# A third output buffer, lent from the matrix products' PSUM banks, for the convolution tiles in a fused backward pass

## The chip, the core and the metric

The kernel runs on one core of a Trainium2 chip. Its time is that of one execution on the device in microseconds, and what is compared are medians of several executions. A profile comes from one more execution that the hardware profiler recorded; "the profile" and "the trace" below are of that one.

## What is computed

The reference is the vector-Jacobian product of a block with two branches that run on one layer-normed input. One is a long convolution over time (2048 steps, 1024 channels) with gates, the other a gated MLP with F = 3584:

```python
xn = layernorm(q)                                   # q: [1, 2048, 1024]
# convolution branch
k_shift = sum of k shifted by t steps times shift_k[:, 3 - t], t = 0..3
kv = k_shift * v
y  = irfft(rfft(kv, padded) * rfft(ssm_k, padded))[:S] + kv * ssm_D
A  = xn * y
# MLP branch
B  = (relu(xn @ W_gate) * (xn @ W_up)) @ W_down
out = q + A + B
# outputs: out and the gradients by q, k, v, shift_k, ssm_k, ssm_D, W_gate, W_up, W_down
```

The kernel returns ten tensors in bfloat16: the forward output and nine gradients.

## The kernel before

**Two recorders on one queue.** Class `LnMlp` writes down the MLP branch and class `ABranch` the convolution branch. Both are Python generators. `LnMlp` yields after each small group of matmuls, with the nanoseconds that the group is worth (1730 for eight 128x512 matmuls in the weight gradients). The loop at the end of the kernel function subtracts these from `left`, and whenever `left` is used up it lets the convolution branch record its next slot and adds the slot's own cost: 1900 in the first stage; in the weight gradients 1900 if the slot holds matmuls and 1250 if not (`SLOT`, `DENSE`, L529). So the order of TensorE's queue is fixed by a budget of nanoseconds and not by what is ready. `A_START` (L777) is what has to pass before the convolution branch begins.

**The stages.**

1. `hidden` (L1046): layer norm, then fourteen blocks (two halves of the rows, seven blocks of 512 columns of F). Each block has eight row tiles, for which gate, up and the gradient of the hidden layer are formed, 8 matmuls each (tiles `ps_g`, `ps_u`, `ps_h`). SyncE loads the blocks of weights (`wg`, `wu`, `wdT`) and stores `h_d` and `ug_d`, in one queue with the convolution's loads and stores.
2. `grad_down` (L1363, tiles `ps_d`) and `grad_in` (L1403, tiles `ps_w`): the weight gradients, sums over 16 row tiles. `gemm16` (L1317) makes one output tile of 16 matmuls and yields after 8 and after 16; its caller then records the copy to SBUF on ScalarE. In three places `four` (L1325) works on four output tiles at once.
3. `out_phase` (tiles `ps_o`): the forward output, from `wd` and transposed rows of the hidden layer (`hT`).
4. `grad_x` (tiles `ps_x`): the gradient by q.

**The convolution branch** runs beside stages 1 and 2. It takes eight groups of 128 channels one after another. Long transforms are done as two rounds of small matmuls with tables of sines (`R`, `FW` forwards; `IA`, `RB` backwards), a VectorE transpose (`flip`) between the rounds, and complex products on VectorE (`cmul`). `slots` (L626) yields pairs: what TensorE does in a slot, and what VectorE does. A run of convolution matmuls that stands between two matmuls of the MLP branch is called a pass below. The small matmuls use parts of the array side by side: `FW` and `RB` 64 rows by 32 columns, `IA` and `R` 32 by 64. Each pass fills one or more PSUM tiles, and ScalarE empties each of them into SBUF (`act`, L74; in the profile its line is L76, and that of the small matmuls L72).

**PSUM.** It has eight banks of 128x512 float32. The matrix products rotate through four single banks (pool `b_ps`, `ps_tile`, L834). The convolution has two tiles of two banks each (pool `a_ps`, tag `aps`), so a third tile waits until the first has been emptied. All its steps (`fwd1_filter`, `fwd1`, `fwd2`, `fwd2_pair`, `inv_a`, `inv_a_pair`, `inv_b`, `inv_b_chan`, `tap_sums`, L330 to L510) take their tiles from there, and a pass fills two of them (in `tap_sums` one).

When the convolution branch has ended, its SBUF is released and `open_right` loads `wd` for stage 3.

Of the kernel before, what the change touches and what calls it, by code (L numbers as in the profile page):

```python
# [12 lines left out]
F32 = mybir.dt.float32  # L13
# [35 lines left out]
class ABranch:  # L49
# [5 lines left out]
    def __init__(self, tc, pri, S, D, k, v, g, shift_k, ssm_k, ssm_D, xn_d, y_d, sk_d, out_gk, out_gv, out_gsk,  # L55
                 out_gh, out_gsD):
        assert S == 2048 and D % P == 0
        self.tc, self.nc, self.pri = tc, tc.nc, pri
        self.S, self.D, self.NG = S, D, D // P
        self.k, self.v, self.g, self.shift_k, self.ssm_k, self.ssm_D = k, v, g, shift_k, ssm_k, ssm_D  # L60
        self.xn_d, self.y_d, self.sk_d = xn_d, y_d, sk_d
        self.out_gk, self.out_gv, self.out_gsk, self.out_gh, self.out_gsD = out_gk, out_gv, out_gsk, out_gh, out_gsD
        self.pools, self.pin, self.dense, self.queue = [], False, False, []

    def pool(self, name, bufs, **kw):
        p = self.tc.alloc_tile_pool(name=name, bufs=bufs, **kw)
        self.pools.append(p)
        return p

# [260 lines left out]
    def fwd1_filter(self, st):  # L330

        B, hn = self.Bh, st["hn"]
        for k in range(2):
            for x in range(2):
                ps = self.ps.tile([P, 2, 512], F32, name="ps0", tag="aps")
                for b in range(2):
                    rows = slice(64 * x + 32 * b, 64 * x + 32 * b + 32)
                    for h in range(2):
                        self.mm(ps[64 * h:64 * h + 64, b], self.R[rows].rearrange("p a l -> p (a l)"),
                                hn[rows, h, 16 * k:16 * k + 16, :].rearrange("p c n -> p (c n)"))  # L340
                self.act(B[:, :, x, 8 * k:8 * k + 8],
                         ps[:].rearrange("p b (cp i n) -> p b cp n i", i=2, n=NB1))
            yield
# [7 lines left out]
    def fwd1(self, B, src):  # L351
        for r0 in range(0, 16, 8):
            for u in range(2):
                ps = self.ps.tile([P, 2, 8, 64], F32, name="ps1", tag="aps")
                for b in range(2):
                    rows = slice(64 * u + 32 * b, 64 * u + 32 * b + 32)
                    for h in range(2):
                        self.mm(ps[64 * h:64 * h + 64, b], self.R[rows].rearrange("p a l -> p (a l)"),
                                src[rows, r0:r0 + 8, 64 * h:64 * h + 64])
                self.act(B[:, :, :, u, r0:r0 + 8, :], ps[:].rearrange("p b r (cp i) -> p b cp r i", i=2))  # L360
            yield

    def fwd2(self, F, half):
        Bf = self.flp[:, half]
        for j0 in range(0, 4, 2):
            for j in range(j0, j0 + 2):
                ps = self.ps.tile([P, 2, 2, 2, 2, 64], F32, name="ps2", tag="aps")
                for ri in range(2):
                    for m in range(2):
                        for q in range(4):  # L370
                            for e in range(2):
                                rows, l = slice(64 * e, 64 * e + 64), 8 * q + 2 * j + m
                                self.mm(ps[32 * q:32 * q + 32, e, :, ri, m, :], self.FW[rows, l, ri, :],
                                        Bf[rows, l, :].rearrange("p (b c) -> p b c", b=2))
                self.act(F[:, 2 * j:2 * j + 2].rearrange("p e b i c -> p (e b i c)"),
                         ps[:].rearrange("p e b i m c -> p (e b i m c)"))
            yield

    def fwd2_pair(self):

        for j in range(4):
            ps = [self.ps.tile([P, 2, 2, 2, 2, 64], F32, name="ps2", tag="aps") for _ in range(2)]
            for m in range(2):
                for ri in range(2):
                    for q in range(4):
                        for e in range(2):
                            rows, l = slice(64 * e, 64 * e + 64), 8 * q + 2 * j + m
                            self.mm(ps[e][32 * q:32 * q + 32, m, :, :, ri, :], self.FW[rows, l, ri, :],
                                    self.flp[rows, :, l, :].rearrange("p k (b c) -> p b k c", b=2))
            for e in range(2):  # L390
                self.act(self.GK[:, 2 * j + e].rearrange("p b k i (m c) -> p (b k i) m c", m=2),
                         ps[e][:].rearrange("p m b k i c -> p (b k i) m c"))
            yield

# [26 lines left out]
    def inv_a(self):  # L421
        C, Q = self.Cg, self.GKV
        for j0 in range(0, 4, 2):
            ps = [self.ps.tile([P, 2, 2, 2, 2, 64], F32, name="ps3", tag="aps") for _ in range(2)]
            for j in range(2):
                for m in range(2):
                    for ri in range(2):
                        for q in range(4):
                            for e in range(2):
                                rows, x = slice(32 * q, 32 * q + 32), 2 * (j0 + j) + m  # L430
                                self.mm(ps[q // 2][64 * e:64 * e + 64, q % 2, j, m],
                                        self.IA[rows, x, ri].rearrange("p a n -> p (a n)"),
                                        Q[rows, 2 * (j0 + j) + e, :, ri, 64 * m:64 * m + 64],
                                        start=ri == 0, stop=ri == 1)
            for h in range(2):
                self.act(C[:, :, 2 * h:2 * h + 2, 2 * j0:2 * j0 + 4, :],
                         ps[h][:].rearrange("p q j m b (cp i) -> p (b cp) q (j m) i", i=2))
            yield

    def inv_a_pair(self):  # L440

        for j in range(4):
            ps = [self.ps.tile([P, 2, 2, 2, 2, 64], F32, name="ps3", tag="aps") for _ in range(2)]
            for m in range(2):
                for ri in range(2):
                    for q in range(4):
                        for e in range(2):
                            rows, x = slice(32 * q, 32 * q + 32), 2 * j + m
                            self.mm(ps[q // 2][64 * e:64 * e + 64, q % 2, m].rearrange("p k b c -> p b k c"),
                                    self.IA[rows, x, ri].rearrange("p a n -> p (a n)"),  # L450
                                    self.GK[rows, 2 * j + e, :, :, ri, 64 * m:64 * m + 64],
                                    start=ri == 0, stop=ri == 1)
            for h in range(2):
                self.act(self.Cs[:, :, 2 * h:2 * h + 2, 2 * j:2 * j + 2, :],
                         ps[h][:].rearrange("p q m k b (cp i) -> p (k b cp) q m i", i=2))
            yield

    def inv_b(self, st, key, half):
        dst, Cf = self.ttile(key), self.flp[:, half]
        st[key] = dst  # L460
        for j in range(2):
            ps = self.ps.tile([P, 2, 8, 64], F32, name="ps4", tag="aps")
            for q in range(4):
                for e in range(2):
                    rows, n0 = slice(64 * e, 64 * e + 64), 16 * (q // 2) + 8 * j
                    self.mm(ps[32 * q:32 * q + 32, e], self.RB[rows, e, :],
                            Cf[rows, n0:n0 + 8, 64 * (q % 2):64 * (q % 2) + 64])
            self.act(dst[:, 8 * j:8 * j + 8, :].rearrange("p r (h c) -> p r h c", h=2),
                     ps[:].rearrange("p h r c -> p r h c"))
        yield  # L470

    def inv_b_chan(self, st, half):
# [3 lines left out]
        for n0 in range(0, NB1, 16):  # L476
            ps = self.ps.tile([P, 16, 64], F32, name="ps5", tag="aps")
            for n in range(16):
                self.mm(ps[:, n, :], Cf[:, n0 + n, :], self.RB[:].rearrange("p h n -> p (h n)"))
            self.act(dv[:, :, n0:n0 + 16], ps[:].rearrange("p n2 n1 -> p n1 n2"))  # L480
# [17 lines left out]
    def tap_sums(self, st):  # L498

        gks, kp = st["gks"], st["kp"]  # L500
        ps = self.ps.tile([P, 2, 512], F32, name="ps6", tag="aps")
        pd = ps[:, 0, 0:P].rearrange("p (i c) -> p i c", i=4)
# [11 lines left out]
    def both(self, *fs):  # L514
# [3 lines left out]
        return go  # L518

# [11 lines left out]
    def steps(self):  # L531
# [25 lines left out]
        for st in self.sts:  # L557
            for p, d in self.slots(st, st["gi"]):
                self.run(p)
# [198 lines left out]

    def small_outputs(self):
# [17 lines left out]
A_START = 45_000  # L777


class LnMlp:  # L780
# [536 lines left out]
    def gemm16(self, ps, lhsT, rhs):  # L1317
        for st in range(self.ST):
            self.pri.pin(self.nc.tensor.matmul(ps[:], lhsT=lhsT(st), rhs=rhs(st), start=(st == 0),  # L1319
                                               stop=(st == self.ST - 1)))  # L1320
            if st % 8 == 7:
# [41 lines left out]
    def grad_down(self, xn_d, ug_d, h_d, out_wd):  # L1363
# [9 lines left out]
        for fb in range(self.FB):  # L1373
# [5 lines left out]
            for j in range(4):  # L1379
                self.pri.now()  # L1380
                if j - 1 in whole:
                    continue
                if j in whole:
# [4 lines left out]
                else:  # L1388
                    wo = [self.e2_tile("wo")]
                    for ob in range(2):  # L1390
                        ps = self.ps_tile("ps_d")
                        yield from self.gemm16(ps, lambda st: hs(st)[:, j * P:(j + 1) * P],
                                               lambda st: gn[st][:, ob * 512:ob * 512 + 512])
                        self.pri.pin(nc.scalar.copy(out=wo[0][:, ob, :], in_=ps[:]))
# [8 lines left out]
    def grad_in(self, ug_d, out_wg, out_wu):  # L1403
        nc, xn, nxt = self.nc, self.xn_nat, self.ugs
        turns = [(fb, w) for fb in range(self.FB) for w in (1, 0)]
        for k, (fb, w) in enumerate(turns):
# [3 lines left out]
            for dp in range(self.DT // 2):  # L1410
# [10 lines left out]
                else:  # L1421
                    wo = [self.e2_tile("wi")]
                    for d in range(2):
                        dc = 2 * dp + d
                        ps = self.ps_tile("ps_w")
                        yield from self.gemm16(ps, lambda st: xn[st][:, dc * P:(dc + 1) * P], sl)
                        self.pri.pin(nc.scalar.copy(out=wo[0][:, d, :], in_=ps[:]))
# [154 lines left out]
def kernel(  # L1582
# [42 lines left out]
    a.identA = b.ident  # L1625
# [66 lines left out]
```

## Time and profile before

| | us |
|---|---|
| median of four executions | 1880.68 (1880.13 to 1881.44) |
| the profiled execution | 1881.13 |
| its span, first to last instruction | 1879.4 |
| `hidden` (to 645.5) | 645.5 |
| `grad_down`, `grad_in` (to 1295.65) | 650.2 |
| `out_phase` (to 1483.07) | 187.4 |
| `grad_x` (to 1879.4) | 396.3 |
| first and last convolution matmul | 110.5 and 1224.1 |

The granted TensorE clock was 1.000 throughout. In the profile, a line such as `PE L72 MATMUL ps<-arena,IA 32*64 32x256 bf16 x32` reads: TensorE, line 72 of the kernel, a matmul from `arena` and `IA` into the tile `ps`, in array tiles of 32 rows by 64 columns, with 32 rows and 256 columns of moving data, 32 times. Matmuls overlap: the mean duration of a 128x512 one is given as 379 ns, while one starts every 0.216 us where nothing disturbs. So starts are compared here, not durations. In a table of windows the columns are the busy time of PE, PE's weight loads, DVE, ACT and POOL (in brackets the number of instructions), then clock, DMA share and GB/s. Idle time in brackets behind a row names what ended it.

### The profile page before, as it was taken

How to read it: one execution, taken by the hardware profiler on the slowest of the kernel's cores; microseconds unless marked ns; L12 is line 12 of the kernel's file. 1: busy time of each engine (PE TensorE's matmuls, PEld its weight loads, DVE VectorE, ACT ScalarE, POOL GpSimd, SP SyncE). 2: the span in 40 equal slices, each digit the busy share in tenths (PEclk: the TensorE clock that was granted, in tenths of full speed). 3: DMA queues.
4: the chain of work that ended last, by engine and by line, in shares of the span. 5: the costliest groups of instructions: out<-in, count | busy, mean ns of one | idle time of the engine just before them, and what ended most of it. 6: DMA issues, size and time to landing. Idle time of an engine off the chain costs nothing.

```text
span 1879.4 us, 32733 instructions
## 1 busy us (share of the span) xinstructions
PE 1871.8 (100%) x13707; PEld 852.2 (45%) x13707; DVE 1049.0 (56%) x1537; ACT 609.4 (32%) x847; POOL 14.8 (1%) x37
## 2 busy tenths in 40 slices
PE   9999999999999999999999999999999999999999
PEld 4444444444444444444444444444444544444444
DVE  6676987888789686575775856600212222222222
ACT  5654454444434445444444454321000000000000
POOL 1000000000000000000000000000000000000000
PEclk9999999999999999999999999999999999999999
DMA  9897689697578666376564452595999955555553
GB/s 248 256 237 171 143 205 233 174 205 179 143 169 223 222 146 170 91 193 192 146 151 139 120 163 74 150 271 161 253 214 258 257 121 124 124 123 123 124 123 73
DMA packets 695509, 323.72 MB, mean 172 GB/s; under 512 B 524864, under 2 KB 664896, under 8 KB 695360
## 3 DMA queue, kind: packets, MB, share of 16 engines
q1 hardware_dynamic: 684864, 300.78, 65.5%
q10 hardware_dynamic: 9216, 16.65, 2.8%
q0 software_dynamic: 1280, 4.20, 0.6%
q8 instruction: 107, 1.75, 0.4%
q14 instruction: 42, 0.34, 0.1%
HBM read 143.79 MB, written 95.44 MB: 127 GB/s over the span
## 4 chain that ended last, share of the span: by engine, by line
PE 98%; DMA 1%; SPq 1%; ACT 0%; issue 0%; DVE 0%
PE ps_x L1550 21%; PE ps_w L1319 20%; PE ps_h L987 10%; PE ps_u L987 10%; PE ps_o L1481 10%; PE ps_g L987 10%; PE ps_d L1319 9%; PE ps L72 5%; PE ps_d L1332 1%; PE ps_w L1332 1%; SPq L1005 1%; DMA goT<-in_grad_out_dram 0%; PE ps_r L1511 0%; DMA wg<-in_B_W_gate_dram 0%; DMA wu<-in_B_W_up_dram 0%; ACT arena L76 0%
## 5 line engine op out<-in xcount | busy, mean ns | idle before, releaser
L1319 PE MATMUL ps_w<-ugs,xn_nat 128*128 128x512 bf16 x1728 | 383.3, 379 | 0.0
L76 ACT CAST arena<-ps 128x1024 bf16<-128x1024 f32 x288 | 277.6, 1017 | 170.6 <-PE ps L72 162.3
L987 PEld LDWEIGHTS <-xnT 128*128 128x128 bf16 x1792 | 170.6, 98 | 210.6 <-issue 11.1
L1319 PEld LDWEIGHTS <-xn_nat 128*128 128x128 bf16 x1728 | 164.3, 98 | 201.3 <-issue 10.2
L327 DVE STREAM_TRANSPOSE arena<-arena 128x1024 f32<-128x1024 f32 x96 | 180.3, 1932 | 118.7 <-ACT arena L76 117.2
L987 PE MATMUL ps_u<-wu,xnT 128*128 128x512 bf16 x896 | 207.1, 379 | 0.7 <-DMA wu<-in_B_W_up_dram 0.7
L987 PE MATMUL ps_h<-wdT,goT 128*128 128x512 bf16 x896 | 205.4, 379 | 1.0 <-DMA goT<-in_grad_out_dram 1.0
L987 PE MATMUL ps_g<-wg,xnT 128*128 128x512 bf16 x896 | 205.3, 379 | 0.4 <-DVE xnT L1031 0.3
L1568 ACT ACTIVATE w<-xn,m 128x512 f32<-128x512 bf16 x32 | 24.3, 807 | 553.3 <-issue 317.5
L1550 PE MATMUL ps_x<-wgT,ggT 128*128 128x512 bf16 x896 | 198.6, 379 | 0.0
L1550 PE MATMUL ps_x<-wuT,guT 128*128 128x512 bf16 x896 | 198.6, 379 | 0.0
L1481 PE MATMUL ps_o<-wd,hT 128*128 128x512 bf16 (+1 forms) x896 | 187.6, 372 | 0.0
L1319 PE MATMUL ps_d<-g_nat,hs 128*128 128x512 bf16 x768 | 171.6, 379 | 0.0
L1550 PEld LDWEIGHTS <-guT 128*128 128x128 bf16 x896 | 87.7, 98 | 105.7
L1550 PEld LDWEIGHTS <-ggT 128*128 128x128 bf16 x896 | 87.7, 98 | 105.5
L987 PEld LDWEIGHTS <-goT 128*128 128x128 bf16 x896 | 85.4, 98 | 105.2 <-issue 3.9
L1481 PEld LDWEIGHTS <-hT 128*128 128x128 bf16 x896 | 87.7, 98 | 99.9
L1552 DVE CUSTOM_DVE_ANT_0 gx<-ps_x,gy 128x512 f32<-128x512 f32 x32 | 22.1, 692 | 185.0 <-PE ps_x L1550 185.0
L1229 ACT CAST gh<-ps_h 128x512 bf16<-128x512 f32 x112 | 65.8, 587 | 180.6 <-PE ps_h L987 168.4
L1102 DVE SCALAR_TENSOR_TENSOR ru<-ru,ps_u 128x512 bf16<-128x512 bf16 x112 | 76.4, 682 | 80.4 <-PE ps_u L987 50.4
L1473 DVE TENSOR_TENSOR ya<-ya,xe 128x1024 bf16<-128x1024 bf16 x16 | 11.1, 692 | 190.0 <-DMA xe<-xn_d 190.0
L80 DVE TENSOR_TENSOR t<-arena 128x2048 bf16<-128x2048 bf16 x96 | 113.8, 1218 | 0.4
(152 smaller groups left out, 1321.3 us busy)
## 6 DMA issues: line engine op xcount, KB each, us to landing
ug_d<-ru SPq DMA_DIRECT2D x112, 256.0 KB
ugs<-ug_d SPq DMA_DIRECT2D x112, 256.0 KB
wg<-in_B_W_gate_dram SPq DMA_DIRECT2D x56, 256.0 KB
wu<-in_B_W_up_dram SPq DMA_DIRECT2D x56, 256.0 KB
h_d<-ht SPq DMA_DIRECT2D x112, 128.0 KB
hs<-h_d SPq DMA_DIRECT2D x56, 256.0 KB
out_dram<-wi SPq DMA_DIRECT2D x56, 256.0 KB
gt<-in_grad_out_dram SPq DMA_DIRECT2D x32, 256.0 KB
```

What stands on the lines that cost most here:

```text
L72: self.pri.pin(self.nc.tensor.matmul(out, lhsT=lhsT, rhs=rhs, start=start, stop=stop))
L76: self.pri.pin(self.nc.scalar.copy(out=out, in_=in_))
L80: self.pri.pin(self.nc.vector.tensor_tensor(out=out, in0=in0, in1=in1, op=op))
L327: self.pri.pin(self.nc.vector.transpose(out=df[:, c0:c0 + 32, :], in_=sf[:, c0:c0 + 32, :]))
L987: self.pri.pin(self.nc.tensor.matmul(ps[:], lhsT=xT[:, kt * P:(kt + 1) * P], rhs=w(kt), start=(kt == 0), stop=(kt == self.DT - 1)), always ...
L1102: return self.pri.pin(nc.vector.scalar_tensor_tensor(out=ru[s][:, 1, :], in0=ru[s][:, 0, :], scalar=0.0, in1=ps[:], op0=ALU.is_gt, op1=ALU ...
L1229: self.pri.pin(nc.scalar.copy(out=gh[:], in_=ps[:]))
L1319: self.pri.pin(self.nc.tensor.matmul(ps[:], lhsT=lhsT(st), rhs=rhs(st), start=(st == 0), stop=(st == self.ST - 1)))
L1332: self.pri.pin(self.nc.tensor.matmul(ps[i][:], lhsT=lhsT(i, st), rhs=rhs(i, st), start=(st == 0), stop=(st == self.ST - 1)))
L1481: nc.tensor.matmul(ps, lhsT=hT[:, kt, :], rhs=self.wd[:, kt, oc], start=(kt == 0), stop=(kt == self.FT - 1))
L1550: nc.tensor.matmul(ps, lhsT=T[:, kt, :], rhs=W[:, kt, oc], start=(i == 0), stop=(i == n - 1))
L1568: nc.scalar.activation(out=w[:, oc], in_=xn[:, oc], func=ACT.Identity, scale=m[:, 7:8], bias=m[:, 6:7])
```

## The change

- **Tiles.** A new function `banks` gives a convolution step its output. While the limit `cap` is 3, every third call takes two single banks from the matrix products' pool (`lend`, which is `ps_tile`, under the name `ps_c`); the other calls take a double-bank tile as before. `evict` empties a double-bank tile with one copy and two single banks with two.
- **Steps.** `fwd2` and `fwd2_pair` are cut into steps of one tile (`f2`, `f2_pair`).
- **Passes.** In the weight gradients a new list of slots (`wide_slots`) is used. It differs from `slots` in two places: the eight steps of `f2_pair` come in slots of three, three and two (limit 3) or four slots of two (limit 2), and the four `f2` steps of the next filter come as three, and as one together with `inv_b` for y. `parts` cuts a slot that asks for more tiles than the limit.
- **Limit.** `cap` starts at 2, becomes 3 after the first `gemm16` of `grad_down`, goes back to 2 in its last block ahead of `four`, and becomes 3 again after the first `gemm16` of `grad_in`.
- **Copies of the products.** `gemm16` records the copy itself, right after its last matmul and ahead of its yield, so it stands ahead of whatever the convolution records there.
- **Start.** `A_START` goes from 45,000 to 60,000.

```diff
+    def banks(self, dims, **sizes):
+        self.turns += 1
+        if self.cap == 3 and self.turns % 3 == 0:
+            parts = [self.lend("ps_c")[:] for _ in range(2)]
+        else:
+            parts = [self.ps.tile([P, 1024], F32, name="ps", tag="aps")[:]]
+        head, n = dims.split()[0], 2 // len(parts)
+        parts = [p.rearrange("p (%s) -> p %s" % (dims, dims), **{head: n}, **sizes) for p in parts]
+        return parts, lambda i: parts[i // n][:, i % n]
+
+    def evict(self, parts, view, out):
+        n = 2 // len(parts)
+        for i, p in enumerate(parts):
+            self.act(out(slice(n * i, n * i + n)), p.rearrange(view))
...
-    def fwd2_pair(self):
-        for j in range(4):
-            ps = [self.ps.tile([P, 2, 2, 2, 2, 64], F32, name="ps2", tag="aps") for _ in range(2)]
...
+    def f2_pair(self, j, m):
+        def go():
+            ps, at = self.banks("e b k i c", b=2, k=2, i=2)
+            for ri in range(2):
+                for q in range(4):
+                    for e in range(2):
+                        rows, l = slice(64 * e, 64 * e + 64), 8 * q + 2 * j + m
+                        self.mm(at(e)[32 * q:32 * q + 32, :, :, ri, :], self.FW[rows, l, ri, :],
+                                self.flp[rows, :, l, :].rearrange("p k (b c) -> p b k c", b=2))
...
+    def parts(self, p):
+        out, left = [[]], self.cap
+        for n, f in p if isinstance(p, list) else [(0, p)]:
+            if n > left:
+                out.append([])
+                left = self.cap
+            out[-1].append(f)
+            left -= n
+        return out
...
-            for p, d in self.slots(st, st["gi"]):
-                self.run(p)
+            for p, d in (self.wide_slots if self.dense else self.slots)(st, st["gi"]):
+                *more, last = self.parts(p)
+                for fs in more:
+                    self.all_of(fs)
+                    yield self.DENSE[0]
+                self.all_of(last)
...
+    def wide_slots(self, st, gi):
+        f2 = [(1, self.f2_pair(j, m)) for j in range(4) for m in range(2)]
+        if self.cap == 3:
+            yield f2[0:3], None
+            yield None, None
+            yield None, None
+            yield f2[3:6], None
...
+        f2H = [] if last else [(1, self.f2(H, 1, j)) for j in range(4)]
+        yield f2H[0:3], tg
...
+        yield f2H[3:4] + [(2, self.inv_b(st, "yt", 0))], tk
...
-A_START = 45_000
+A_START = 60_000
...
-    def gemm16(self, ps, lhsT, rhs):
+    def gemm16(self, ps, lhsT, rhs, out):
         for st in range(self.ST):
             self.pri.pin(self.nc.tensor.matmul(ps[:], lhsT=lhsT(st), rhs=rhs(st), start=(st == 0),
                                                stop=(st == self.ST - 1)))
+            if st == self.ST - 1:
+                self.pri.pin(self.nc.scalar.copy(out=out, in_=ps[:]))
             if st % 8 == 7:
                 yield 1730
...
+                if fb == self.FB - 1 and j == 1:
+                    self.branch.cap = 2
...
+                        if fb == 0 and self.branch.cap == 2:
+                            self.branch.cap = 3
...
+    a.identA, a.lend, b.branch = b.ident, b.ps_tile, a
```

## The prediction

> **What bounds the kernel now.** I read the page first, then the chain that ended last, then the timeline of TensorE and ScalarE around convolution passes.
>
> ```profile
> span 1879.4 us, 32733 instructions
> ...
> PE 1871.8 (100%) x13707; PEld 852.2 (45%) x13707; DVE 1049.0 (56%) x1537; ACT 609.4 (32%) x847; POOL 14.8 (1%) x37
> ...
> PE 98%; DMA 1%; SPq 1%; ACT 0%; issue 0%; DVE 0%
> ```
>
> TensorE is never free, so only what shortens TensorE's own queue counts. A busy PE is not a PE at its peak, though, so I need the price of an undisturbed matmul. The chain has a long stretch of nothing else:
>
> ```profile
> 1483.07 386.77 PE ps_x L1550 x1792
> ```
>
> 386.77 / 1792 = 0.2158 us for one 128x512 step. With that step, a convolution pass in the weight gradients can be priced from the timeline of TensorE (start, duration, instruction):
>
> ```profile
> 784.70 3.63 PE L1319 MATMUL ps_d<-g_nat,hs 128*128 128x512 bf16 x16
> 788.26 0.42 PE L72 MATMUL ps<-hn,R 32*64 32x512 bf16 x8
> 788.61 3.63 PE L1319 MATMUL ps_d<-g_nat,hs 128*128 128x512 bf16 x16
> ```
>
> From 784.70 to 788.61 are 3.91 us: 16 steps (3.45) and 0.46 for the pass. Its eight matmuls run side by side in the 32x64 array tiles, so their work is one step, 0.22. The remaining 0.24 is the way into the other array tiling and back. A 64x32 pass of sixteen 512-column matmuls (803.32, between 792.86 and 803.88) gives 11.02 - 48 x 0.2158 - 2 x 0.2158 = 0.23. So a pass costs its work plus 0.235 us whatever is in it.
>
> The second cost is a wait. Where two passes lie only eight matmuls apart, the chain leaves TensorE:
>
> ```profile
> 815.96 3.02 PE ps_d L1319 x14
> 818.98 0.65 PE ps L72 x32
> 819.63 0.29 issue
> 819.91 1.94 ACT arena L76 x2
> 821.85 0.04 issue
> 821.89 0.63 PE ps L72 x28
> 822.52 2.48 PE ps_d L1319 x11
> ```
>
> The second pass began at 821.32 with four matmuls and stood until 821.89: there are two double-bank tiles, and the second was drained only at 821.85. Comparing each pass of the dense stage (645 to 1296) with the shortest of its kind gives ten such waits, all eight matmuls behind another pass: 0.21, 0.24, 0.28, 0.56, 0.28, 0.28, 0.22, 0.29, 0.28, 0.30 us, together 2.94 us. Outside passes the dense stage has no lost time (its other steps sum to 0.3 us above 0.2158 each).
>
> **Part 1, passes of three tiles.** In the built order of instructions the small-array passes fall from 176 to 170: the spectra of G and K take three passes per group in place of four (four groups, -4); the filter spectrum with the inverse step for y takes two in place of three (three groups, -3), and one group, caught where the limit goes back to two, takes one more. The matmuls are the same 8203 large and the same small ones. A merged pass stays in 64x32 tiles. 6 x 0.235 = -1.4 us. The Trainium skill (TensorE: Matmul & The Clock Gate, Single matmul latency) gives a lone warm matmul a constant of about 166 ns over its columns, which in a stream is hidden; two such exposures per pass would be 0.33 us, and six -2.0 us. The rows say 0.235; I take the rows.
>
> **Part 2, the third buffer.** With two double tiles and every third tile in two lent banks, the second tile of a pass eight matmuls behind another is no longer the one drained last. In the built order nine dense passes stand at most nine matmuls behind another. In five of them one tile is lent or belongs to an older pass, and the other was first to be drained. In two only one tile, or the first-drained one, is needed at once; one (after 4669) begins with a lent tile and needs the last-drained tile 0.5 us later; in one (3637, limit two) both tiles are awaited as before but nine matmuls behind, so some 0.07 us remain. I keep 0.15 us: -2.8 us. Bounds: -2.94 (all gone) and 0 (all come back elsewhere).
>
> What it adds lies on ScalarE. A double tile is one copy, a lent one two:
>
> ```profile
> L76 ACT CAST arena<-ps 128x1024 bf16<-128x1024 f32 x288 | 277.6, 1017 | 170.6 <-PE ps L72 162.3
> ...
> L1229 ACT CAST gh<-ps_h 128x512 bf16<-128x512 f32 x112 | 65.8, 587 | 180.6 <-PE ps_h L987 168.4
> ```
>
> 2 x 587 - 1017 = 157 ns each, for 57 more copies 9 us in a stage where ScalarE has room (ACT is the fourth engine here):
>
> ```profile
> 645.50:864.50 219.00, 218.73 (x2130) 99.22 (x2123) 159.13 (x172) 98.80 (x128) 0.82 (x2) 1.00 0.60 160
> 864.50:1295.65 431.15, 431.14 (x3711) 194.92 (x3709) 237.62 (x258) 173.24 (x229) 0.82 (x2) 1.00 0.53 154
> ```
>
> 272 of 650 us. Against this change stands a rule of the Trainium skill (TensorEngine Tiling (Array Packing), PSUM Bottleneck): packing quickens TensorE but not the emptying of PSUM, and copies should span several tiles, not be cut up. A three-tile pass hangs 2 x 1.02 + 2 x 0.59 = 3.2 us of copies on ScalarE, with one matmul copy 3.8 us, and the next pass can come after 16 matmuls, 3.45 us, plus its predecessor's 0.9. By the rule each of the 14 such passes could delay a successor by up to 0.3 us, 4 us in all, and the gain would be Part 1 alone. By the rows the next pass first needs the tile drained first, about 1.4 us after its pass. I take zero.
>
> The lent banks also bind the matrix products, which have four banks. In the built bank numbers the closest reuse after a lend is eight matmuls (three passes: 3421, 3925, 4581), 1.7 us plus a pass, and there the bank concerned is the one drained first or a product's bank whose copy was queued ahead. Cost 0, bounds 0 and 0.5 us for each. The product's copy now stands in ScalarE's order right behind its last matmul, ahead of the copies of a pass there; those then start up to 0.59 us later. No close pass turns on that: 0, bound +0.3.
>
> VectorE's operations are the same and keep their slots. The tightest cover is the spectrum pass behind the last flips:
>
> ```profile
> 751.66 3.71 DVE L327 STREAM_TRANSPOSE arena<-arena 128x1024 f32<-128x1024 f32 x2 [7.22 <-ACT arena L76]
> ```
>
> They end at 755.37 and the pass starts at 758.4: 3.0 us of cover, with 40 matmuls behind the pass that feeds the flips. In two groups it is now 32, 1.7 us less, so 1.3 us stay: cost 0. If VectorE came more than 1.3 us later, TensorE would wait for the excess, twice.
>
> **Part 3, the later start.** The convolution's first pass moves by 72 matmuls, 15.5 us. In the first stage, the 16 up-projections at 236.38 took 3.94 us against 3.63 for an undisturbed run: 0.31 us of waiting for `wu`, whose loads on SP's queue stood behind two stores of `gv`. In the new order no convolution transfer stands between a block's `wg` and `wu` loads: -0.3 us, bounds -0.3 and +0.6 (two such waits elsewhere). One close pair of passes there stays, with its 0.24 us.
>
> At the end, the last pass comes 88 matmuls later, 19 us, and with it the load of `wd`, the weights of the next stage:
>
> ```profile
> 1262.19 0.47 SPq L1442 DMA_DIRECT2D wd<-in_B_W_down_dram  x1
> ```
>
> ```profile
> 1270.00:1280.00 10.00, 10.00 (x48) 4.56 (x47) 0.00 (x0) 1.76 (x3) 0.00 (x0) 1.00 0.62 229
> 1280.00:1290.00 10.00, 10.00 (x48) 4.53 (x47) 0.00 (x0) 1.76 (x3) 0.00 (x0) 1.00 0.08 26
> ```
>
> The DMA share falls to 0.08 after 1280, so the last piece landed within 17 us. In SP's new order it is issued behind the third-last `wi` store, two stores of 32 matmuls (13.8 us) before the stage begins, and is first read 21 steps (4.5 us) into it: 18 us, just enough. Cost 0, bounds 0 and +2.
>
> **Sum.** -1.4 - 2.8 - 0.3, with 0.1 kept for small new waits: -4.4 us. The profiled execution took 1881.13 us (span 1879.4 and 1.7 around it), so it would become 1876.7; the median shown is 0.45 lower, so 1876.3.
>
> **Rivals.** Forecast (68%): as summed, 1875.3 to 1877.3.
> A (22%): the passes merge, but ScalarE is the true limit and the waits reappear, wholly or by half, behind the longer bursts of copies. For it: every one of the ten waits ended with ScalarE. Against it: ScalarE's 42% and the order of draining. -1.4 - 0.3 is 1879.0; with half of the waits 1877.6.
> B (6%), slower: lent banks make matrix products wait. 58 passes lend; a wait of 0.08 us at each eats the gain, and above 0.14 us the kernel is slower by over 0.2%. At 0.15 it is 1876.3 + 8.7 = 1885. For it: half of the products' banks are away in each. Against it: the reuse distances above.
> C (2%): `wd` lands more than 8 us too late and TensorE idles at 1296: 1884 or more.
> D (2%): more is gained than I see, 1874.
>
> A change under 0.2% (3.8 us) can't be told from none here, so faster means under 1876.9. About nine tenths of the forecast's chance lies there: 0.68 x 0.88 + 0.02 = 0.62. Same: 0.08 + 0.22 = 0.30. Slower: 0.08. The range goes from a full gain, 1875.2, to A, 1879.2; B, C and most of D stay outside.
>
> **What would show it.** 170 small-array passes at unchanged prices (0.46 for eight 512-column matmuls), merged ones at the work plus one 0.235. No passes in the dense stage that start and then stand for 0.2 us or more, and no ScalarE pieces in the chain there; A is right if they are still there. Steps of `ps_d` or `ps_w` over 0.2158 right behind a lending pass speak for B. A gap before the first `ps_o` row or at its 22nd matmul speaks for C. I am wrong in Part 3 if a new gap stands in `ps_u` or `ps_g`.

## The result, and the profile after

| | before | after |
|---|---|---|
| median, us | 1880.29 (53 executions, 1879.2 to 1882.7) | 1876.99 (33 executions, 1875.53 to 1878.28) |
| the profiled execution, us | 1881.13 | 1877.92 |
| its span, us | 1879.4 | 1876.1 |

The ratio is 0.9981, with a 95% interval of 0.9977 to 0.9986: 3.3 us less, about 0.2%. The forecast was 1876.3, in a range of 1875.3 to 1877.3. The prediction called only a time under 1876.9 faster; the median lies 0.1 us above that line, while the interval is clear of no change. The granted clock was 1.000 in all profiles below.

The head of the page after has TensorE at 100% again, 57 more ScalarE instructions (904 for 847) and the same 13707 matmuls. In the chain of waits ScalarE's share is printed as 0%, as before; its ten waits were too small to show there:

```profile
span 1876.1 us, 32801 instructions
...
PE 1869.3 (100%) x13707; PEld 852.8 (45%) x13707; DVE 1049.8 (56%) x1537; ACT 613.4 (33%) x904; POOL 14.8 (1%) x37
...
PE 98%; SPq 1%; DMA 1%; DVE 0%; ACT 0%; issue 0%; ACTq 0%
```

Whether a close pair still waits is seen in the timeline of TensorE. Here a pass lies eight matmuls behind another again, with one lent tile (`ps_c`) in each (columns: start, duration, instruction):

```profile
926.63 0.41 PE L89 MATMUL ps<-hn,R 32*64 32x512 bf16 x4
926.64 0.41 PE L89 MATMUL ps_c<-hn,R 32*64 32x512 bf16 x4
926.98 3.63 PE L1503 MATMUL ps_w<-ugs,xn_nat 128*128 128x512 bf16 x16
```

and the timeline of ScalarE at the same place:

```profile
924.86 1.07 ACT L93 CAST arena<-ps_c 128x512 bf16<-128x512 f32 x2
925.82 1.03 ACT L93 CAST arena<-ps 128x1024 bf16<-128x1024 f32 x1
```

The older pass's double tile was drained only at 926.85, 0.2 us after both tiles of the new pass had begun: it was not needed. The pass took 0.35 us from 926.63 to the next large matmul, the same as one without a neighbour.

To find where the 3.2 us went, I took for every pass the time from its start to the start of the next pass, less 0.2158 us for each large matmul between, and compared passes of one kind over all traces. The shortest is the price of an undisturbed pass; what is over is a wait. (A pass of small matmuls starts 0.09 us later behind a large matmul than another large one would. The pass of `inv_b_chan`, 128x64 over the whole array, does not, so the pass ahead of it counts 0.09 us less than its like, eight times in every kernel. That is no wait and is left out.) In us:

| kernel | passes undisturbed | waits in `hidden` | waits in the weight gradients |
|---|---|---|---|
| before | 115.3 | 0.62 | 2.98 |
| after | 114.0 | 1.17 | 0.13 |

That is -1.3, +0.55 and -2.85. The time to the first pass, less 0.2158 us for each large matmul and a quarter of it for each transpose of 128 columns, was 11.24 us before and 11.68 after, 0.43 longer. Over the eight profiles with the later start it goes from 10.3 to 12.5, so the 0.43 lies within the scatter (more on it at the tail below). The sum is -3.2, as is the difference between the two profiled executions.

### The profile page after: what moved, and what is told of

The parts are those of the page before. It is cut to its first block, busy times and chain, and to the rows that moved or that the text cites. A ratio compares the mean times of both kernels' runs of the same rounds, so it can differ in the third digit from the quotient of the medians.

```text
span 1876.1 us, 32801 instructions
## 1 busy us (share of the span) xinstructions
PE 1869.3 (100%) x13707; PEld 852.8 (45%) x13707; DVE 1049.8 (56%) x1537; ACT 613.4 (33%) x904; POOL 14.8 (1%) x37
## 4 chain that ended last, share of the span: by engine, by line
PE 98%; SPq 1%; DMA 1%; DVE 0%; ACT 0%; issue 0%; ACTq 0%
PE ps_x L1739 21%; PE ps_w L1503 20%; PE ps_h L1171 10%; PE ps_o L1670 10%; PE ps_u L1171 10%; PE ps_g L1171 10%; PE ps_d L1503 9%; PE ps L89 4%; PE ps_d L1518 2%; PE ps_c L89 1%; SPq L1189 1%; PE ps_w L1518 1%; DMA goT<-in_grad_out_dram 0%; PE ps_r L1700 0%; DMA wg<-in_B_W_gate_dram 0%; DMA ug_d<-ru 0%
## 5 line engine op out<-in xcount | busy, mean ns | idle before, releaser
L93 ACT CAST arena<-ps 128x1024 bf16<-128x1024 f32 x240 | 234.2, 1021 | 72.3 <-PE ps L89 63.0
L1506 ACT CAST wi<-ps_w 128x512 bf16<-128x512 f32 x108 | 63.9, 592 | 200.4 <-PE ps_w L1503 183.0
L97 DVE TENSOR_TENSOR t<-arena 128x2048 bf16<-128x2048 bf16 x96 | 114.0, 1218 | 0.4
```

The lines of the kernel that those rows point to most:

```text
L93: self.pri.pin(self.nc.scalar.copy(out=out, in_=in_))
L97: self.pri.pin(self.nc.vector.tensor_tensor(out=out, in0=in0, in1=in1, op=op))
L1506: self.pri.pin(self.nc.scalar.copy(out=out, in_=ps[:]))
```

## The experiments

The theory is the prediction's own, in parts: the merged passes give some 1.3 us, the third buffer takes the waits out of the weight gradients, and the later start is worth nothing, or costs a little. First rival: the later start alone spaces the passes differently and so removes the waits. Second rival: tile-by-tile spectra or the earlier copy of the products does it, and the lent banks are not needed. Third: lending has a price for the large matmuls that eats part of the gain.

**Only the later start**, on the kernel before:

```diff
-A_START = 45_000
+A_START = 60_000
```

> The kernel before with the convolution's start at 60,000 and nothing else: 176 passes, every later one 56 to 72 matmuls further back. Theory (the shift is only a phase: it removes one wait for the up weights and may add small waits of passes in the first stage): within 0.5 us of the kernel before, about ten waits of the second tile in the weight gradients, 2 to 3 us together, still there. Rival (the shift is what gained): 2 us or more faster, and the waits in the weight gradients fewer. If the five new waits of passes in the first stage (1.2 us in the changed kernel against 0.3 before) come from the shift, they are here too.

It took 1880.75 us against 1880.91 for before in the same series, ratio 0.9998 (0.9990 to 1.0007). Its waits are 1.04 us in `hidden` (+0.4) and 2.1 in the weight gradients (-0.9, eight waits in place of ten). So the start does move passes out of each other's way there and into it elsewhere, and the net effect can't be told from none. The first rival falls.

**All but lending and merging:** the later start, spectra in steps of one tile, and the copy of a product right behind its last matmul, with the old slots and no lent bank.

```diff
-            for p, d in (self.wide_slots if self.dense else self.slots)(st, st["gi"]):
+            for p, d in self.slots(st, st["gi"]):
...
-                            self.branch.cap = 3
+                            self.branch.cap = 2
...
-                        self.branch.cap = 3
+                        self.branch.cap = 2
```

> The changed kernel without lent banks and with the old list of slots: passes stand exactly where those of e1_start60 stand; what is left of the change is the later start, spectra tile by tile and the product's copy right behind its last matmul. Theory: within 0.3 us of e1_start60, waits in the weight gradients 2 to 3 us. Rival (the earlier copy of the products or the tile-by-tile steps carry part of the gain): 1 us or more faster than e1_start60 and fewer waits.

1879.50 us, ratio 0.9996 (0.9988 to 1.0004). Waits in the weight gradients: 1.36, where 2 to 3 had been expected. Against the run before, three waits of 0.277 us in spectrum passes are gone and one of 0.29 has become 0.38: a pass that fills its two tiles one after the other needs the second one later than a pass that writes both in turn. This I had not counted as an effect of its own. That it is the order of the tiles and not the earlier copy of the products is argued: this run changed both, and the copy alone is tried further below, in the whole change only.

**Lending without merging:** as above, with the limit at 3, so that every third tile is lent.

```diff
-                            self.branch.cap = 2
+                            self.branch.cap = 3
...
-                        self.branch.cap = 2
+                        self.branch.cap = 3
```

> Like e3_nolend with the lent banks, still at most two tiles in a pass: 176 passes at the same places, about 59 of them with a lent tile. Theory (the third buffer takes away the wait of the second tile): 2.5 to 2.9 us faster than e3_nolend, waits in the weight gradients under 0.3 us. Rival (lent banks delay matrix products or ScalarE becomes the limit): less than 1.5 us faster, with waits at other places. The changed kernel should then be another 1.3 us faster by its merged passes.

1878.60 us, ratio 0.9987 (0.9981 to 0.9994). Waits in the weight gradients: 0.05. From the run above to this one only lending differs: -1.31 us of waits. That is half of the 2.5 to 2.9 us expected, since the run above had already lost the other half. The medians differ by 0.9 us and their intervals overlap; it is the waits that show the effect. To the whole change only merging is left: the undisturbed passes go from 115.3 to 114.0.

**The whole change with the old start:**

```diff
-A_START = 60_000
+A_START = 45_000
```

> The changed kernel with the old start of 45,000: theory (third buffer and merged passes carry the gain, the start is a phase): within 0.6 us of the changed kernel either way, the small waits of passes in the first stage back to about 0.3 us and the wait for the up weights back at about 0.3 us. Rival (the start matters): slower than the changed kernel by 1 us or more.

1877.53 us, ratio 0.9980 (0.9974 to 0.9987); its interval and that of after overlap almost wholly. Waits: 0.62 in `hidden`, as much as before, and 0.24 in the weight gradients, of which 0.21 stand at a close pair that lies ahead of the point where the limit becomes 3. So the waits of the old order go without the later start. No run adds lending alone to the kernel before, where a pass still writes its two tiles in turn, so how much of the 2.85 us the third buffer would clear by itself is not shown; it is 1.3 where only merging is still to come.

**Merging without the third buffer:**

```diff
-        if self.cap == 3 and self.turns % 3 == 0:
+        if False:
```

> The changed kernel with its 170 passes at the same places and three tiles in 14 of them, but no lent bank: the third tile of a pass has to wait until ScalarE has emptied the first. Theory: in each such pass the third tile is due about 0.5 us after the pass begins and its tile is free at about 1.5 us, so 0.9 to 1.0 us of wait in each of 14, 13 us in all, and the waits of close pairs return besides: 1890 us or more. Rival (merging alone pays and the lent banks are decoration): no slower than the changed kernel by over 2 us.

1893.74 us, ratio 1.0071 (1.0059 to 1.0084), 16.8 above after. All 14 passes of three tiles wait. The same pass in the timeline of TensorE, first without lending:

```profile
745.09 0.42 PE L89 MATMUL ps<-arena,FW 64*32 64x128 bf16 x32
745.34 0.44 PE L89 MATMUL ps<-arena,RB 64*32 64x512 bf16 x8
746.75 0.41 PE L89 MATMUL ps<-arena,RB 64*32 64x512 bf16 x8 [0.96 <-ACT arena L93]
747.32 1.03 PE L1503 MATMUL ps_d<-g_nat,hs 128*128 128x512 bf16 x4 [0.16 <-issue]
```

then in the kernel after:

```profile
745.39 0.42 PE L89 MATMUL ps_c<-arena,FW 64*32 64x128 bf16 x32
745.64 0.66 PE L89 MATMUL ps<-arena,RB 64*32 64x512 bf16 x16
746.23 2.98 PE L1503 MATMUL ps_d<-g_nat,hs 128*128 128x512 bf16 x13
```

Without lending the third tile must wait until the first one of the same pass has been written, copied for 1.02 us and set free: 0.96 us of idle TensorE. The summary of what TensorE waited for, over all passes of this kernel, has it as `ACT arena L93: 13.3, 14` (us, times); in the kernel after that list is empty.

**The copy of the products back behind the yield:**

```diff
-            if st == self.ST - 1:
-                self.pri.pin(self.nc.scalar.copy(out=out, in_=ps[:]))
             if st % 8 == 7:
                 yield 1730
+        self.pri.pin(self.nc.scalar.copy(out=out, in_=ps[:]))
```

> The changed kernel with the product's copy recorded after the yield, so behind the copies of a pass at that place, as in the kernel before. Theory (nothing turns on that order): within 0.3 us in the sum of waits. Rival (the early copy is what keeps the four banks free for lending): waits at lent tiles or at the first product matmul behind a pass, 1 us or more together.

1877.06 us, ratio 0.9981 (0.9973 to 0.9988), no different from after. In the weight gradients one wait of 0.11 us is new, one of 0.05 is gone and one of 0.08 is as it was: 0.19 for 0.13. The copy's place is worth nothing that can be measured.

**Lending in the first stage too** (a flag `early`, true until the weight gradients begin; passes and limit otherwise unchanged):

```diff
-        if self.cap == 3 and self.turns % 3 == 0:
+        if (self.cap == 3 or self.early) and self.turns % 3 == 0:
```

> The changed kernel with lent banks in the first stage too, 48 more passes that lend. There the matrix products fill a bank every 8 matmuls, 1.7 us, so the four banks come round twice as fast as in the weight gradients. If lending has a price where banks turn fast (the slower rival of the prediction), gaps appear in ps_g, ps_u, ps_h behind lending passes: over 0.1 us at each of 48 would be 5 us slower. Theory, from the bank distances of the weight gradients halved: waits of close pairs go (0.4 us and 0.24 us), few new gaps, within 1 us of the changed kernel.

1877.21 us, ratio 0.9982 (0.9974 to 0.9989). Four waits of passes in `hidden` (0.38, 0.29, 0.24 and one of two of 0.13 us) are gone, but the sum stays at 1.25 us (1.17 in after), since a new one of 0.91 us has come, and here it is a large matmul that waits. Timeline of TensorE:

```profile
545.57 1.89 PE L1171 MATMUL ps_h<-wdT,goT 128*128 128x512 bf16 x8 [0.32 <-DVE ru L1286]
547.84 1.46 PE L1171 MATMUL ps_h<-wdT,goT 128*128 128x512 bf16 x6 [0.38 <-DVE ru L1286]
```

The two rows show 0.70 of it as idle time. The pass ahead of them, at 544.63, holds a lent tile. The releaser in brackets is VectorE's `ru`, which reads the up-projection out of its bank and stood behind operations of the convolution: with two of the four product banks lent, `ps_h` has to take a bank that VectorE has not emptied yet (`ps_h` reads nothing that VectorE writes there; that the two share a bank is argued from this). At the same place in the kernel after, without a lent tile, `ps_h` did not wait. This is the mechanism of rival B, once in the 48 passes that lend there. In the weight gradients, where ScalarE alone empties the product banks and has time, it did not occur.

**More merging:** the four tiles of the first filter round, and those of the gate gradient's first round, no longer go as two passes of two. The first joins the inverse step ahead of it, the other three make one pass: 162 passes in place of 170.

```diff
-        yield iaG, q
+        yield [(2, iaG)] + f1h[0:1] * wide, q
...
-        yield f1h, q
+        yield (f1h[1:4] if wide else f1h[0:2]) or None, q
```

> The changed kernel with two more merges per group in the weight gradients: the first filter tile goes into the first inverse pass of the 32x64 array tiling, the other three into one pass; the same for the gradient's tiles in the second pair of inverse passes. 162 passes in place of 170. Theory (a merged pass saves 0.17 to 0.22 us): 1.4 to 1.9 us off the cost of the passes, 0.07 to 0.1% faster than the changed kernel if no new waits come. Rival (longer passes wait for their third buffer or VectorE): no gain, with waits of over 1 us together inside the longer passes.

1876.07 us, ratio 0.9978 (0.9968 to 0.9987): below both kernels, though its interval overlaps that of after (0.9977 to 0.9986). Undisturbed passes 113.5 (-0.44), waits 1.10 and 0.00. Eight passes fewer should have given eight times 0.2 us. What took it back: in the pair of tiles of a filter pass the four matmuls of one tile and the four of the other run side by side, on different rows of the array. Three tiles alone are two steps, and the fourth, with the inverse step, is one: three steps where two pairs took two. From the prices: 0.785 + 2 x 0.447 = 1.68 before the merge, 0.978 + 0.650 = 1.63 after it, 0.05 us for a pass.

**More merging with the old start:**

```diff
-A_START = 60_000
+A_START = 45_000
```

> The kernel with more merged passes (162), and the start put back to 45,000. Theory: the later start does nothing for the gain; it only shifts where in the first stage two close pairs of passes and one wait for VectorE fall, which cost about 0.5 us more there than with the old start, and the third buffer clears the dense stage from either start. Then this is some 0.5 us below the run with more merged passes and the start of 60,000 (1876.07), about 1875.6, ratio 0.9975, with 0.9 us of hidden waits in place of 1.4. Rival: the merged passes of the old start meet other neighbours (the first filter tile now stands in one pass with an inverse step) and waits return in the dense stage: 1876.5 or more, with dense waits above 0.6 us in the sum.

1878.23 us, ratio 0.9988 (0.9982 to 0.9995). My theory expected 1875.6 and is refuted for this kernel; the rival has it, dense waits included (2.4 us). `hidden` did shrink to 0.43. The kernel has 165 passes here, since one group fewer falls where the limit is three. Where the two merged passes follow each other after eight matmuls, the second one stops at its third tile. TensorE:

```profile
780.09 1.90 PE L1532 MATMUL ps_d<-g_nat,hs 128*128 128x512 bf16 x8
781.92 0.41 PE L89 MATMUL ps<-hn,R 32*64 32x512 bf16 x4
781.94 0.41 PE L89 MATMUL ps_c<-hn,R 32*64 32x512 bf16 x4
782.93 0.41 PE L89 MATMUL ps<-hn,R 32*64 32x512 bf16 x4 [0.59 <-ACT arena L93]
```

ScalarE at the same time, with the three tiles of the first pass in its order:

```profile
779.97 1.01 ACT L93 CAST arena<-ps 128x1024 bf16<-128x1024 f32 x1 [1.80 <-PE ps_c L89]
780.88 1.08 ACT L93 CAST arena<-ps_c 128x512 bf16<-128x512 f32 x2
781.84 1.04 ACT L93 CAST arena<-ps 128x1024 bf16<-128x1024 f32 x1
```

The third copy ends at 782.88 and the third tile starts at 782.93. With the start of 60,000 the same two passes lie 16 matmuls apart:

```profile
791.69 0.41 PE L89 MATMUL ps<-hn,R 32*64 32x512 bf16 x4
792.03 3.63 PE L1532 MATMUL ps_d<-g_nat,hs 128*128 128x512 bf16 x15
795.59 0.41 PE L89 MATMUL ps<-hn,R 32*64 32x512 bf16 x4
795.60 0.41 PE L89 MATMUL ps_c<-hn,R 32*64 32x512 bf16 x4
795.83 0.38 PE L89 MATMUL ps<-hn,R 32*64 32x512 bf16 x4
```

(The trace lacks one record of these 16.) Two such pairs lost 0.79 and 0.78 us, one ahead of the limit's rise 0.21, and 0.6 us went to a late load of `xn_nat` at the turn to `grad_in`, whose cause I did not trace. So here the phase of the start is worth some 2 us, with that load in it, where in the change as made it was worth nothing. What prediction and theory had in rival A, ScalarE's bursts as the limit, is real at eight matmuls between two passes of three tiles; the change as made has no such pair.

## Why the forecast was nearly right, step by step

**Part 1, merging.** Expected -1.41 for six passes, measured -1.3; the rows were the right choice against the constant of the Trainium skill (TensorE: Matmul & The Clock Gate, Single matmul latency), about 166 ns, from which the estimate was -2.0. The sentence that a pass costs its work plus 0.235 us "whatever is in it" is not quite true. The prices of undisturbed passes, in us, from the start of the last large matmul ahead to that of the first behind, less one step (counted from pass to pass, as above, most are 0.01 more):

| pass | one tile | two tiles | three tiles |
|---|---|---|---|
| spectra of G and K, 16 matmuls of 256 columns a tile | - | 0.657 | 0.875 |
| filter spectrum, 32 matmuls of 128 columns a tile | 0.443 | 0.776 | 1.093 |

In the first row a tile is its work, 0.22, and the pass 0.22 on top: -4 x 0.22. In the second a further tile costs 0.32 to 0.33, half as much again as its work. Three groups went from 2 x 0.776 + 0.651 (two filter passes and one for y) to 1.093 + 0.936: -0.174 each and not -0.235; the step for y costs 0.07 more behind the small matmuls. The group that was split went from 0.776 to 2 x 0.443, +0.11 and not +0.235. Sum: -0.88 - 0.52 + 0.11 = -1.29.

**Part 2, the third buffer.** Expected -2.8 with 0.15 left; measured -2.85 with 0.13 left, 0.08 of it at the pair at 3637, for which 0.07 was written down. The mechanism is the one named, but not the only one: 0.9 of it came from the new phase in the run with the later start alone, and 0.75 more with tile-by-tile spectra, both without a third buffer.

**What lending adds on ScalarE.** Nothing on the path, as expected. The price, 157 ns for an extra copy, was too high even as busy time: ScalarE's rose by 4.0 us, 70 ns for each of 57. Two mean durations had been added, but two copies in a row overlap: `x2` took 1.07 us at 924.86, against 1.03 for one double tile. By the prediction's own sums the copies of a three-tile pass were no limit either: 3.8 us of them against 3.45 + 0.9 to the next pass, so the 0.3 us of delay set down for rival A doesn't follow from them. The rule of the Trainium skill (TensorEngine Tiling (Array Packing), PSUM Bottleneck), that the PSUM copy may become the bottleneck, named a danger that did not bind here, at ScalarE's 43% in the weight gradients (282.6 of 650.3 us). In the kernel with three-tile passes and no third buffer, and in pairs of three-tile passes, it does bind.

**Lent banks, copy order, VectorE's cover: 0.** All three hold: no large matmul in the weight gradients waits, the copy's place changed nothing, and no spectrum pass waited for flips. Rival B is refuted for this stage.

**Part 3, the later start.** This step failed: -0.3 was expected, +0.55 came, just within the bound of +0.6. In all, -4.4 was expected and the medians give -3.3 (-2.6 to -4.3 by the interval). Of the 1.1 between them, 0.85 is this step, less the 0.1 that had been kept for small waits; Part 1 and Part 2 together are off by less than 0.1, and the rest, some 0.3, is within the interval. That the median still fell into the range is in part luck. The forecast set out from the 1880.68 of four executions, and the 53 gave 1880.29; the same gain from 1880.68 would be 1877.4, just outside. Nor does the time alone tell the forecast from rival A with half of the waits (1877.6), as the interval reaches to 1877.7. The traces do, with 0.13 us of waits where that rival has 1.5.

The gain of Part 3 was there: the 16 up-projections that had waited for `wu` took 3.62 us (at 235.34) in place of 3.94.

But "one close pair of passes there stays" was wrong, as there are two, and one pass met a late VectorE. The timeline of TensorE has the new close pair and the late VectorE, and neither wait is shown as idle time, but as a pass too long for its matmuls (0.80 for 0.42, 0.93 for 0.64):

```profile
155.33 0.80 PE L89 MATMUL ps<-gt,R 32*64 32x512 bf16 x8
...
252.09 0.93 PE L89 MATMUL ps<-arena,IA 32*64 32x256 bf16 x32
```

In the first, four matmuls start at 155.33 and the other four at 155.72; ScalarE emptied the second tile of the pass before until 155.67:

```profile
153.75 1.92 ACT L93 CAST arena<-ps 128x1024 bf16<-128x1024 f32 x2
```

The second stood at its second tile, which `tap_sums` had filled and VectorE had yet to read, behind the gate gradient and the MLP's own work:

```profile
249.86 1.22 DVE L97 TENSOR_TENSOR gt<-gt,xt 128x2048 bf16<-128x2048 bf16 x1
250.99 0.68 DVE L1286 SCALAR_TENSOR_TENSOR ru<-ru,ps_u 128x512 bf16<-128x512 bf16 x1
251.71 0.43 DVE L1292 TENSOR_TENSOR ht<-ru 128x512 bf16<-128x512 bf16 x1
252.05 0.28 DVE L97 TENSOR_TENSOR dg<-ps,ident 128x128 f32<-128x128 f32 x1
```

`dg` ends at 252.33 and the pass goes on at 252.39. The two cost 0.38 and 0.29 us, two smaller ones 0.13 each, while 0.31 (`wu`) and 0.07 are gone. All but one of the small ones stand in the run with only the later start too, and the run of the whole change with the old start has the 0.62 us of before: they come with the phase and not with the other parts of the change. I had counted close pairs with care in the weight gradients and only glanced at the first stage.

**The tail.** `wd` is in time: the first 55 matmuls of the next stage take 12.03 us, 55 x 0.2158 = 11.87 and the usual end.

```profile
1292.28 12.03 PE L1670 MATMUL ps_o<-wd,hT 128*128 128x512 bf16 x55
```

Open: the first 110 us differ by up to 2.4 us between the profiled executions, more than any part of the change but the waits. In the profile of after, two waits stand there that before has not:

```profile
47.69 1.89 PE L1171 MATMUL ps_h<-wdT,goT 128*128 128x512 bf16 x8 [0.92 <-ACT ru L1279]
49.95 1.24 PE L1171 MATMUL ps_h<-wdT,goT 128*128 128x512 bf16 x5 [0.37 <-ACT ru L1279]
```

ScalarE's `ru` itself waited for a store of `ug_d`. The profile of before has others, 0.65 us for `wu` near 10 us and 0.96 for `goT` near 25. Waits of this kind near 50 us came to 0 to 1.3 us in the eight profiles with the start of 60,000 and to 0 to 0.3 in the three with 45,000, so a few tenths of them may belong to the later start; these profiles don't settle it.

## What to carry to other kernels

Where two streams share TensorE's queue, shifting one against the other by a few matmuls moves every wait in both. List the pairs of steps that lie closer than their buffers take to drain, in all stages, before giving a shift a price. A third buffer makes such pairs harmless, and it is what makes a longer pass possible at all: with two, merging cost 16.8 us. And what a merged pass saves is the way in and out, 0.2 us, only if the matmuls in it still run side by side as they did.

## What the runs showed of the hardware

- Small matmuls side by side have a rate of their own: in passes of 32, 64 and 96 of 128 columns each further 32 took 0.33 and 0.32 us, 10 ns a matmul, where their columns would take 0.22. Sixteen of 256 columns took 0.22, 13.6 ns each, with no such excess.
- A pass of 64x32 or 32x64 matmuls started 0.31 us after the last large matmul ahead of it, where the next large one, or a pass of 128x64 over the whole array, starts after 0.22.
- Two consecutive ScalarE copies of 128x512, 0.59 us each by their durations, took 1.07 together.
- A TensorE row with no idle time shown can hold a wait: in the pass at 155.33 the first matmuls last 0.40 us each, so the 0.39 us to the start of the others shows no gap, only a row of 0.80 us where 0.42 is usual.
